# Twelve more blocks of the second product as three rounded products, and another order of the first 41 blocks' steps

## The chip, the cores and the metric

One core of a Trainium2 chip runs the whole program. The metric is the device time of one execution in microseconds (us). The kernel before takes 478.98 us, the median of three executions (477.38 to 479.07 us).

## What is computed

A gated recurrence over 768 positions for 4 batches and 8 heads of size 40 gives a matrix x of 3072 tokens by 320. A two-layer network follows: x times w_in (320 by 2048), a smooth ReLU, and the result times w_out (2048 by 320). Cut to what matters:

```python
m_new = np.maximum(f_gate[:, :, t] + m, i_gate[:, :, t])
C = f_stab * C + i_stab * np.einsum('bhd,bhe->bhde', vt, kt)
n = f_stab * n + i_stab * kt
y[:, :, t] = o * np.einsum('bhde,bhe->bhd', C, qt) / np.maximum(np.abs(nq), 1.0)
...
h = x @ w_in
g = np.where(h >= 1, h, np.where(h <= -1, 0.0, (h + 1) ** 2 / 4))
return (g @ w_out).astype(np.float32)
```

## The kernel before

**The recurrence in sequences.** The recurrence is cut into 24 sequences n (6 chunks of 128 positions times 4 batches; sequence n is chunk n // 4 of batch n % 4). For each of them TensorE multiplies queries and keys (`score_mm`, step C, tile `raw`), ScalarE makes the decays (`decay`, D, tile `Abc`), VectorE multiplies the two (`score_mul`, c), TensorE takes the product with the values (`values_mm`, U), and VectorE adds the part that comes from the state (`values_add`, u, tile `hv`), makes the normalizer (z, three small instructions), the gated result (s and y, tiles `sz` and `y`; for four sequences GpSimd does these as t and n). TensorE turns the result (T, tiles `ident,y`), ScalarE and VectorE write its high and low parts (x, and w with two instructions, tiles `xh` and `xl`). The state is kept beside it: K on TensorE (`v,vk`, or `ow` in the first chunk), k, i and a on VectorE (tile `C`, and `hv<-psa,G` for i), I on TensorE (`C,qn`), e, E, v and S on GpSimd.

**The network in blocks.** Four sequences make a group of 512 tokens, and 16 blocks of 128 hidden columns belong to each group, which makes 96 blocks x. `mm1` (step M, tile `psh`) is 8 products of 512 columns (7 where `narrow` has done one), in a rounded float32 format with a high and a low part of both sides. ScalarE and VectorE make the ReLU in three steps (R and q on ScalarE, r, which is `sharpen`, on VectorE, tile `r`). `mm2` (step N, tile `pso`) is the second product: for each of the four 128-token tiles either one plain float32 product of `rs` and `of`, or three rounded ones with `gh`, `gl` and `oh`, `ol`. `gh` is made by ScalarE (`high`, step G) and `gl` by VectorE (`low`, step g). Which of the two it is depends on whether step G has run for the block:

```python
        if x in gh:
            prod = [(gh[x], oh[:, fc, :]), (gh[x], ol[i][:, k, :]), (gl[x], oh[:, fc, :])]
        else:
            prod = [(rs[x], of[i][:, k, :])]
```

In the kernel before the first G in the order is G16, so blocks 0 to 15 (the whole first group) are plain and 80 blocks are split.

**The weights.** They arrive as 64-bit numbers in 16 pieces of two blocks each and are put into float32 by `convert`, whose steps are the digits 1 (ScalarE, tile `mg`), 2 and 5 (VectorE), 3 (GpSimd), 6 (ScalarE, the high part, `wh` or `oh`) and 7 (VectorE, the low part, `wl` or `ow`). The number behind the digit is the piece: 0, 1, 3, 5, 7, 9, 11, 13 are of w_in (tiles `win`), 2, 4, 6, 8, 10, 12, 14, 15 of w_out (tile `ow`). A split second product needs steps 6 and 7 of its w_out piece, a plain one needs steps 1 to 5 alone.

**What sets the order.** The text ORDER lists all steps by hand; every engine runs its part of them in that order (class `InOrder`), with waits only where data need them. "+n" behind a step puts n products of zeros, which compute nothing, ahead of its first TensorE instruction (`hot`). `ps_h` has two buffers, so M of a block waits for r of the block two M before it. `wk`, `mo` and `ow` are pools of buffers in SBUF; `stage` holds the pieces in work and is closed before the pool `late` opens at the first step p.

Of the kernel before, what the change touches and what calls it, by code (L numbers as in the profile page):

```python
# [42 lines left out]
15 35 B8 c4.1 P1 v5 55 R4 L6 S5 q4 r4 Q5 D5.1 N2 65 16 c4.0 75 26 L7 36 A6 D5.0 B9 q5 L8 N3 Z1 U4 u4 z4 L10 r5 t4 n4
M6 R6 C5 q6 E5 56 27 S6 17 c5.1 N4 T4 x4 66 I5 c5.0 r6 37 M7 e4 w4 57 I6 i6 A7 D6.0 Q6 e6 V7 N5 K5 R7 67 i5 28 38 S7
L9 77 D6.1 210 U5 a4 M8 E6 310 q7 18 r7 D7.0 M9 C6 Q7 u5 z5 64 k5 58 A9 L11 R8 q8 e5 c6.1 N6 L12 c6.0 110 510 t5 a5 U6
29 r8 n5 D7.1 H0 u6 T5 R9 62 19 N7 39 x5 59 69 v6 K6 z6 V8 t6 v7 q9 w5 L13 79 k6 a6 A8 N8 L14 C7 M10 211 c7.0 A10 111
r9 E7 c7.1 311 n6 511 M11 R10 Q9 V9 611 112 610 212 711 I7 T6 R11 312 i7 q10 Q8 S8 x6 N9 213 q11 113 U7 M12 M13 512
r10 w6 u7 e7 D8.1 E8 313 R12 r11 q12 L15 513 613 K7 X6 68 N10 R13 N11 k7 X4 z7 t7 I8 713 114 n7 T7 V10 q13 v8 S10 M14
R14 214 M15 314 x7 S9 r12 q14 r13 514 N12 N13 i8 614 r14 w7 I9 72 215 K8 D9.1 M16 315 115 515 N14 i9 74 M17 X5 R15 X7
76 p8 78 q15 r15 R16 a7 D8.0 612 C8 q16 k8 615 710 712 r16 N15 P2 c8.1 D10.1 M18.1 R17 c8.0 e9 O0.0 G16 O0.1 D10.0  # L50
o0.1 q17 m8 b8 o0.0 J9.18 D9.0 g16 R18 l8 r17 G17 M19 Q10 U8 N16 c9.0 c9.1 O0.2 q18 r18 R19 e8 M20.1 O0.3 m9 b9 q19
714 E9 j10.20 r19 u8 g17 G18 Z2 N17 Q12 p9 z8 l9 M21 R20 q20 c10.1 G19 v9 c10.0 A11 U9 s8 a8 v10 y8 K9 E10 M22 o0.2
r20 o0.3 V11 I10 715 R21 q21 k9 u9 r21 T8 x8 G20 z9 g18 R22 Q11 M23 A12 N18 R23 g19 p10 l10 m10 G21 i10 w8 g20 q22 q23
r22 N19 G22 b10 a9 I11 e11 S11 e10 A13 U10 g22 N20 g21 E11 s9 r23 M24 u10 D11.1 D11.0 z10 N21 G23 X8 R24 s10 y9 q24
y10 M25 r24 i11 G24 S13 g23 T9 R25 g24 N22 x9 S12 q25 w9 X9 D13.0 r25 K10 N23 k10 v11 V12 a10 G25 D12.0 g25 J11.26 N24
D12.1 c11.0 c11.1 U11 K11 u11 E12 N25 z11 V13 v12 k11 A14 s11 T10 p12 P3 M26 x10 y11 l12 D13.1 w10 X10 a11 T11 M27 x11
R26 w11 X11 q26 I12 R27 r26 I13 S14 q27 i12 M28.1 i13 G26 r27 e12 D14.0 g26 e13 j12.28 G27 M29 c12.0 Q13 R28 g27 Q14
q28 c12.1 Z3 N26 r28 m12 M30 b12 G28 N27 R29 g28 q29 K12 R30 r29 N28 v13 V14 q30 k12 G29 a12 M31 g29 r30 G30 N29 R31
g30 q31 M32 r31 G31 g31 I14 R32 M33 e14 q32 D14.1 r32 U12 G32 M34 R33 u12 E13 g32 q33 z12 N30 R34 r33 q34 s12 p13 M35
G33 r34 l13 g33 y12 N31 R35 i14 q35 r35 M36.1 O1.3 O1.2 G34 o1.3 o1.2 g34 j13.36 R36 q36 M37 c13.1 Q15 O1.1 c13.0 o1.1  # L60
O1.0 T12 R37 m13 o1.0 N32 q37 r36 b13 x12 r37 K13 G35 w12 X12 N33 V15 k13 v14 g35 U13 G37 a13 g37 K14 E14 u13 N34 k14
V16 z13 A15 v15 A16 p14 I15 G36 s13 N35 l14 g36 e15 y13 M38 a14 i15 N36 R38 q38 S15 r38 M39.1 G38 D15.1 g38 S16 j14.39
R39 M40 c14.1 Q16 q39 c14.0 D16.1 r39 T13 m14 K15 R40 M41 v16 k15 q40 b14 x13 r40 N37 R41 w13 X13 q41 D15.0 r41 U14
N38 u14 E15 G40 z14 G39 V17 D16.0 g40 J15.42 g39 M42 G41 s14 Q17 c15.1 A17 c15.0 N39 R42 g41 q42 y14 a15 U15 r42 T14
u15 E16 A18 M43 x14 z15 S17 w14 X14 s15 I16 R43 y15 P4 M44 e16 q43 i16 D17.1 r43 p16 S18 T15 M45.1 x15 R44 w15 X15 l16
q44 J16.45 R45 r44 q45 N40 c16.0 Q18 Z4 r45 c16.1 M46 m16 N41 b16 G43 G42 g43 M47 G44 g42 D18.0 g44 N42 R46 q46 U16
R47 r46 q47 N43 u16 E17 A19 D18.1 r47 z16 M48 p17 G46 s16 l17 G47 g46 D17.0 N44 g47 S19 R48 M49.1 q48 G45 r48 D19.1
g45 j17.49 M50 c17.0 Q20 R49 c17.1 q49 m17 N45 R50 q50 r49 b17 r50 K16 M51 k16 V18 v17 N46 R51 q51 r51 M52 G48 a16 g48
N47 R52 q52 M53 r52 O2.3 O2.1 o2.3 G49 o2.1 G51 g49 I17 M54.1 e17 g51 R53 i17 q53 O2.0 D19.0 J18.54 r53 o2.0 O2.2 M55
H1 o2.2 Q19 c18.0 c18.1 N48 H2 H3 H4 U17 G50 y16 H5 g50 N49 E18 u17 R55 z17 R54 A21 I18 s17 q55 N50 i18 e18 G52 y17  # L70
q54 g52 H6 T16 r54 K17 x16 H7 M56 v18 V19 k17 H8 S21 H9 w16 X16 N51 R56 H10 a17 q56 r55 K18 G54 H11 M57 G53 V20 k18
v19 g54 g53 N52 H12 R57 r56 q57 I19 G56 r57 N53 e19 g56 i19 M58 N54 M59 G55 G57 g55 g57 R58 T17 H13 N55 x17 q58 w17
X17 H14 r58 R59 K19 p18 N56 q59 m18 l18 D21.1 r59 b18 M60 G58 G59 g58 N57 R60 g59 q60 a18 D21.0 r60 U18 k19 N58 a19
E19 G60 u18 V21 g60 M61.1 A20 z18 s18 y18 j19.61 R61 q61 M62 c19.1 c19.0 r61 U19 R62 G61 S20 q62 g61 T18 A22 M63 x18
r62 E21 D20.1 w18 X18 u19 N59 p21 R63 z19 l21 q63 s19 D20.0 I21 r63 P5 N60 S22 y19 G63 i21 D22.1 g63 C20 N61 c20.1 Q22
G62 c20.0 Q23 D22.0 g62 T19 I20 x19 N62 i20 Z5 w19 X19 M64 N63 R64 q64 M65.1 O3.2 O3.1 r64 o3.1 o3.2 G64 j22.65 R65
g64 q65 M66 c22.1 Q21 r65 O3.3 O3.0 M67 R66 c22.0 o3.0 o3.3 q66 G65 r66 N64 R67 g65 q67 G66 r67 J21.68 g66 G67 N65
c21.1 c21.0 g67 M68 m21 N66 R68 b21 q68 r68 M69 G68 g68 N67 R69 q69 r69 M70 G69 g69 N68 R70 q70 r70 M71 G70 g70 N69
R71 q71 r71 U21 G71 N70 u21 E20 g71 V22 z21 M72 V23 p20 A23 s21 l20 m20 N71 R72 y21 q72 b20 r72 M73 G72 g72 U20 R73
q73 M74 u20 E22 r73 z20 S23 G73 I22 R74 p22 T21 g73 l22 M75 x21 s20 q74 w21 X21 D23.0 y20 N72 i22 R75 m22 q75 T20 N73  # L80
r74 b22 x20 r75 G74 w20 X20 G75 M76 g74 D23.1 g75 U22 R76 q76 M77.1 u22 E23 r76 z22 G76 j23.77 R77 g76 q77 s22 M78
c23.1 c23.0 r77 N74 R78 y22 q78 r78 M79 G77 g77 I23 R79 T22 i23 q79 N75 x22 r79 w22 X22 U23 G78 g78 N76 u23 z23 s23
N77 G79 y23 g79 T23 N78 x23 w23 X23 M80 N79 R80 q80 r80 M81 O4.1 O4.2 G80 o4.1 o4.2 g80 M82 R81 q81 r81 O4.3 R82 M83
# [846 lines left out]
```

## Time and profile before

| | |
|---|---|
| median of three executions | 478.98 us |
| the profiled execution | 479.52 us, of it span 477.7 us |
| TensorE (PE) busy | 468.7 us, 98% of the span |
| VectorE (DVE) busy | 322.5 us, 68% |
| ScalarE (ACT) busy | 286.5 us, 60% |
| GpSimd (POOL) busy | 154.3 us, 32% |
| granted TensorE clock | 1.0 in all 40 slices |
| DMA | 51.69 MB, mean 108 GB/s |

A row of the profile names an instruction by what it writes and reads: `gl<-r,gh` is the low part of step g, `pso<-ow,r` a plain second product (two records for each), `pso<-oh,gh`, `pso<-ow,gh` and `pso<-oh,gl` the three products of a split one. All rows have the helper's line L111, so they are told apart by tiles. A TensorE record lasts longer than the engine needs for it, since products overlap; what one costs in a stream is the distance from its start to the next one's.

### The profile page before, as it was taken

Reading aid. Unit: us, or ns where it says so; the run is one execution under the profiler, and the core shown is the slowest. Engines: PE = TensorE matmul, PEld = TensorE weight load, DVE = VectorE, ACT = ScalarE, POOL = GpSimd, SP = SyncE. Lnnn points to the kernel's source line nnn. Section 1 sums busy time; section 2 is a strip of 40 time slices with the busy share of each in tenths; the row PEclk is TensorE's granted clock in tenths of the full one; section 3 lists DMA queues with packets and bytes.
Section 4 is the critical chain, followed back from the end, with each engine's and each line's share of the span. In section 5 each row is a group of like instructions: output and inputs, shape, how many; then the busy total and the mean of one; then the engine's idle time right before and its main releaser. Section 6 shows DMA issues by size and latency. Waiting matters only on the chain.

```text
span 477.7 us, 8809 instructions
## 1 busy us (share of the span) xinstructions
PE 468.7 (98%) x3399; PEld 404.6 (85%) x3399; DVE 322.5 (68%) x582; ACT 286.5 (60%) x559; POOL 154.3 (32%) x175
## 2 busy tenths in 40 slices
...
GB/s 267 296 206 274 244 199 284 214 198 94 96 113 112 45 174 67 2 128 132 81 162 29 73 72 102 89 0 128 116 127 0 89 1 1 1 56 0 1 0 56
DMA packets 25433, 51.69 MB, mean 108 GB/s; under 512 B 8312, under 2 KB 14896, under 8 KB 25392
## 3 DMA queue, kind: packets, MB, share of 16 engines
...
## 4 chain that ended last, share of the span: by engine, by line
PE 91%; DVE 6%; DMA 1%; issue 1%; POOL 1%; ACT 0%; SPq 0%; DVEq 0%; POOLq 0%
PE pso L111 38%; PE psh L111 37%; PE psa L111 16%; DMA ident<-in_cst 1%; DVE win L111 1%; DVE C L111 1%; DVE z L111 1%; POOL fi_s L111 1%; DVE xl L111 0%; DVE y L111 0%; DVE r L111 0%; DVE xh L111 0%; DVE sz L111 0%; DVE hv L111 0%; ACT r L111 0%
## 5 line engine op out<-in xcount | busy, mean ns | idle before, releaser
L111 ACT ACTIVATE r<-psh,half 128x512 f32<-128x512 f32 x96 | 65.8, 686 | 90.4 <-PE psh L111 87.8
L111 PE MATMUL psh<-xh,wh 128*128 128x512 f32 x288 | 102.8, 411 | 1.2 <-DVE r L111 0.8
L111 PE MATMUL pso<-oh,gh 128*128 128x320 f32 x320 | 101.7, 318 | 0.0
L111 DVE SCALAR_TENSOR_TENSOR r<-psh,r 128x512 f32<-128x512 f32 x96 | 65.7, 686 | 52.3 <-ACT r L111 51.6
L111 PE MATMUL pso<-ow,gh 128*128 128x320 f32 x320 | 99.0, 309 | 0.0
L111 PE MATMUL pso<-oh,gl 128*128 128x320 f32 x320 | 98.8, 309 | 0.0
L111 PE MATMUL psh<-xh,wl 128*128 128x512 f32 (+1 forms) x274 | 94.0, 400 | 0.0
L111 DVE TENSOR_TENSOR gl<-r,gh 128x512 fp32r<-128x512 f32 x80 | 62.4, 791 | 28.0 <-ACT gh L111 27.8
L111 ACT CAST gh<-r 128x512 fp32r<-128x512 f32 x80 | 48.7, 616 | 46.2 <-DVE r L111 25.6
L111 PEld LDWEIGHTS pso<-oh,gh 128*128 128x128 f32 x320 | 60.2, 188 | 3.1 <-issue 0.5
L111 PEld LDWEIGHTS pso<-ow,gh 128*128 128x128 f32 x320 | 60.3, 188 | 2.0
L111 ACT ACTIVATE r<-r 128x512 f32<-128x512 f32 x96 | 60.5, 631 | 2.3
L111 PEld LDWEIGHTS psh<-xh,wl 128*128 128x128 f32 (+1 forms) x274 | 51.3, 188 | 12.1 <-DVE wl L111 0.2
L111 PE MATMUL psh<-xl,wh 128*128 128x512 f32 x192 | 60.6, 397 | 0.0
L111 PEld LDWEIGHTS pso<-oh,gl 128*128 128x128 f32 x320 | 60.1, 188 | 0.0
L111 PEld LDWEIGHTS psh<-xh,wh 128*128 128x128 f32 x288 | 49.2, 189 | 9.8 <-DVE r L111 2.0
L111 ACT ACTIVATE Abc<-Abc,nA 128x128 f32<-128x128 f32 x160 | 50.7, 390 | 2.5 <-POOL Abc L111 2.3
L111 POOL TENSOR_TENSOR v<-vk,G 128x328 f32<-128x328 f32 x36 | 29.6, 825 | 64.9 <-PE psa L111 45.2
L111 POOL TENSOR_TENSOR m<-m 128x1024 bf16<-128x1024 f32 x12 | 24.2, 2017 | 60.4 <-DVE m L111 50.7
L111 PEld LDWEIGHTS psh<-xl,wh 128*128 128x128 f32 x192 | 36.1, 188 | 8.9 <-DVE xl L111 0.4
L111 DVE TENSOR_TENSOR Abc<-psa,Abc 128x512 f32<-128x512 f32 x43 | 28.1, 684 | 15.6 <-PE psa L111 15.3
L111 PE MATMUL pso<-ow,r 128*128 128x320 f32 x128 | 36.9, 436 | 0.0
...
## 6 DMA issues: line engine op xcount, KB each, us to landing
...
```

The lines of the kernel that those rows point to most:

```text
L111: r = getattr(self.engine, name)(*args, **kwargs)
```

## The change

Blocks 0 to 3 stay plain; blocks 4 to 15 get steps G and g, and with them the split second product. The w_out pieces from the third on get their float32 form in one buffer of `stage` in place of one of `ow` each, since only the high and low parts are used later. To make room, the single gate chunk of later on (steps H) shares its tiles with the batch of gates before it, and `dx` shares one with `ex`. The order of the steps is another one up to `c16.0 Q18`, between M45 and M46; behind it both texts are the same. The instructions that are added are 12 `gh` casts on ScalarE and 12 `gl` subtractions on VectorE; on TensorE 48 plain products become 144 rounded ones, and 32 products of zeros become 26. No conversion, transfer or step of the recurrence is added or left out.

```diff
@@
-SPLIT_FROM = 8
+PLAIN = 2
@@ def gate_sums(c):
-        new = lambda name, p, n=L: pool.tile([p, n], F32, name=name if c else name + "0", bufs=1)
+        def new(name, p, n=L):
+            if c and name != "ex":
+                shared = pool.tile([P, NB * L + 1 if name == "m" else L], F32, name={"m": "m_s"}.get(name, name + "_u"), bufs=1)
+                return shared[:p, :n]
+            return pool.tile([p, n], F32, name=name if c else name + "0", bufs=1)
+
@@ def batch_exps():
-        batch["dx"] = later.tile([P, D], F32, name="dx", bufs=1)
+        batch["dx"] = later.tile([P, L], F32, name="ex", bufs=1)[:, :D]
@@ def convert(k, nw):
             if k == 2:
-                w["out"] = of[i] = ow.tile([P, 656], F32, name="ow")[:, :2 * DM].rearrange("p (k e) -> p k e", k=2)
+                if i < PLAIN:
+                    of[i] = ow.tile([P, 656], F32, name="ow")[:, :2 * DM]
+                else:
+                    of[i] = stage.tile([P, 2 * DM], F32, name="wout", bufs=1)
+                w["out"] = of[i] = of[i].rearrange("p (k e) -> p k e", k=2)
@@ ORDER
...
-v2 w3 11 Lc K1 M0 V4 21 F R0 31 k0 B4 V3 B5 K2 k1 51 q0 M1 k2 61 v3 I4 L2 R1 r0 q1 71 22 32 r1 B6 A4 B7 i4 M2 12 52 M3
-K3 R2 L3 23 v4 k3 A5 R3 33 13 53 K4 q2 N0 L4 E4 63 q3 N1 r2 S4 D4.0 73 M4 D4.1 k4 r3 24 V5 M5 L5 14 C4 34 54 25 R5 V6
...
+K2 s3 y3 B4 B5 w2 T3 w0 x3 L2 w3 V3 12 61 V4 w1 F A4 M0 R0 k0 B6 q0 B7 L3 v3 k1 22 M1 k2 P1 32 v4 R1 q1 r0 I4 Z1 71 52
+23 A5 K3 r1 L4 M3 k3 S4 N0 13 M2 i4 33 53 24 Q4 R3 q3 r3 N1 L5 63 K4 L6 R2 q2 14 34 E4 S5 73 54 A6 D4.1 k4 Q5 25 L7 r2
...
```

**First place: VectorE ahead of the first block.** The rows show VectorE's queue at the end of the front, where the low parts of the first four turned results (`xl`, `xh`) are made, which the first M needs. Before:

```order
L111 TENSOR_TENSOR y<-pso,sz 128x320
L111 TENSOR_TENSOR xl<-psa,xh 128x2x128
...
L111 TENSOR_TENSOR xl<-pso,xh 128x2x128
L111 TENSOR_TENSOR xh<-pso,xh 64x128
L111 TENSOR_SCALAR win<-wraw 128x768
L111 TENSOR_TENSOR C<-psh,cs 120x369
L111 SCALAR_TENSOR_TENSOR fi_s<-fi_s,ah_u 128x128
L111 SCALAR_TENSOR_TENSOR ah_u<-rst,fi_s 128x128
L111 TENSOR_TENSOR C<-pso,cs 120x369
L111 SCALAR_TENSOR_TENSOR win<-mg,win 128x768
```

In the change:

```order
L112 TENSOR_SCALAR win<-wraw 128x768
L112 TENSOR_TENSOR A_295<-pso,A_295 128x512
...
L112 TENSOR_TENSOR y<-pso,sz 128x320
L112 SCALAR_TENSOR_TENSOR win<-mg,win 128x768
...
L112 TENSOR_TENSOR y<-psa,sz 128x320
L112 SCALAR_TENSOR_TENSOR fi_s<-fi_s,ah_u 128x128
L112 SCALAR_TENSOR_TENSOR ah_u<-rst,fi_s 128x128
L112 TENSOR_TENSOR xl<-psh,xh 128x2x128
L112 TENSOR_TENSOR xh<-psh,xh 64x128
```

The two VectorE steps of weight piece 1 (21 and 51, tile `win`) and the gate sums of step B4 (`fi_s`, `ah_u`) stand ahead of the low parts now; they stood behind them.

**Second place: TensorE around blocks 4 and 5.** The rows show second products among first products, values and turns. Before:

```order
L111 MATMUL psa<-raw 128x128 x8
L111 MATMUL pso<-ow,r 128x320 x4
L111 MATMUL psa<-v_925,Abc 128x41 x8
L111 MATMUL psa<-ident,y 128x128 x3
L111 MATMUL pso<-ow,r 128x320 x4
```

In the change:

```order
L112 MATMUL psa<-raw 128x128 x8
L112 MATMUL pso<-oh,gh 128x320
L112 MATMUL pso<-ow,gh 128x320
L112 MATMUL pso<-oh,gl 128x320
...
L112 MATMUL psa<-v_980,Abc 128x41 x8
L112 MATMUL psa<-ident,y 128x128 x3
```

Where four plain products stood for a block, twelve rounded ones stand (three for each of the four token tiles).

**Third place: VectorE behind the values of sequence 5.** The rows begin with step u5 (`hv<-psa,hv`) in both. Before:

```order
L111 TENSOR_TENSOR hv<-psa,hv 128x328
L111 SCALAR_TENSOR_TENSOR z<-hv,G 128x8
L111 TENSOR_TENSOR z<-z,hv 128x8
L111 RECIPROCAL z<-z 128x8
L111 TENSOR_TENSOR C<-psa,cs 120x369
L111 SCALAR_TENSOR_TENSOR ow<-mg,ow 128x640
L111 TENSOR_TENSOR Abc<-psa,Abc 128x512 x2
L111 SCALAR_TENSOR_TENSOR ow<-mg,ow 128x640
L111 TENSOR_TENSOR C<-C 120x369
L111 TENSOR_SCALAR win<-wraw 128x768
```

In the change:

```order
L112 TENSOR_TENSOR hv<-psa,hv 128x328
L112 TENSOR_SCALAR wout<-wraw 128x640
L112 TENSOR_TENSOR C<-psa,cs 120x369
...
L112 TENSOR_TENSOR gl<-r,gh 128x512
L112 TENSOR_TENSOR Abc<-psa,Abc 128x512
...
L112 SCALAR_TENSOR_TENSOR wout<-mg,wout 128x640
...
L112 TENSOR_TENSOR ow<-wout,oh 128x640
L112 TENSOR_TENSOR gl<-r,gh 128x512
```

The subtractions `gl` and the low parts of w_out (`ow<-wout,oh`) stand among the same work of the recurrence, where before only steps 2 and 5 of w_out stood; before, the steps 7 of w_out came some ten blocks later.

## Rows read from the trace of the kernel before

**Rows 1.** The page: busy time by engine, and the chain that ended last.

```profile
PE 468.7 (98%) x3399; PEld 404.6 (85%) x3399; DVE 322.5 (68%) x582; ACT 286.5 (60%) x559; POOL 154.3 (32%) x175
...
PE 91%; DVE 6%; DMA 1%; issue 1%; POOL 1%; ACT 0%; SPq 0%; DVEq 0%; POOLq 0%
```

**Rows 2.** Stretches: length, busy us (x instructions) of PE, PEld, DVE, ACT, POOL, clock, DMA.

```profile
66.30:91.50 25.20, 25.07 (x155) 19.92 (x154) 22.12 (x36) 16.20 (x34) 16.24 (x17) 1.00 0.80 262
...
130.00:157.90 27.90, 27.90 (x258) 25.14 (x257) 26.45 (x44) 16.62 (x29) 16.79 (x15) 1.00 0.34 100
42.00:130.00 88.00, 87.87 (x534) 68.86 (x533) 66.89 (x110) 62.60 (x128) 49.76 (x49) 1.00 0.65 204
```

**Rows 3.** Timeline (start us, us), two plain second products, then I, K and a first product.

```profile
108.88 4.47 PE L111 MATMUL pso<-ow,r 128*128 128x320 f32 x16
113.19 0.79 PE L111 MATMUL psa<-C,qn 120*128 120x123 f32 x6
113.82 0.83 PE L111 MATMUL psa<-v,vk 128*120 128x123 f32 x6
114.41 0.48 PE L111 MATMUL psh<-xh,wh 128*128 128x512 f32 x1
```

**Rows 4.** Timeline: a split second product, a first product, the next split one.

```profile
441.44 0.31 PE L111 MATMUL pso<-oh,gh 128*128 128x320 f32 x1
...
443.19 0.63 PE L111 MATMUL psh<-xh,wh 128*128 128x512 f32 x2
...
445.06 0.31 PE L111 MATMUL pso<-oh,gh 128*128 128x320 f32 x1
```

**Rows 5.** Timeline of VectorE and TensorE where the first blocks begin.

```profile
31.73 0.29 DVE L111 TENSOR_TENSOR xh<-pso,xh 64x128 fp32r<-64x128 f32 x1
32.05 0.62 DVE L111 TENSOR_SCALAR win<-wraw 128x768 uint16<-128x768 uint16 x1
...
32.79 0.79 PE L111 MATMUL psa<-ow 128*120 128x123 f32 x6
33.16 0.28 DVE L111 SCALAR_TENSOR_TENSOR fi_s<-fi_s,ah_u 128x128 f32<-128x128 f32 x1
33.39 0.70 PE L111 MATMUL psh<-xh,wh 128*128 128x512 f32 x2
33.48 0.42 DVE L111 TENSOR_TENSOR_SCAN ah_u<-rst,fi_s 128x128 f32<-128x128 f32 x1
...
34.25 1.07 DVE L111 SCALAR_TENSOR_TENSOR win<-mg,win 128x768 int32<-128x768 int32 x1
...
36.64 0.33 PE L111 MATMUL psa<-ident,fi_s 128*128 128x128 f32 x1 [0.40 <-POOL fi_s L111]
```

**Rows 6.** Timeline: VectorE idle in the front.

```profile
27.14 0.17 DVE L111 SCALAR_TENSOR_TENSOR z<-pso,G 128x8 f32<-128x8 f32 x1 [1.08 <-PE pso L111]
```

**Rows 7.** Timeline: score products (C), values (U), a turn (T) and what follows it.

```profile
10.80 1.16 PE L111 MATMUL psa<-raw 40*128 40x128 f32 x16
...
15.96 1.98 PE L111 MATMUL psa<-ow,Abc 128*128 128x41 f32 x16
...
104.81 0.49 PE L111 MATMUL psa<-ident,y 128*128 128x128 f32 x3
105.05 0.71 PE L111 MATMUL psh<-xh,wh 128*128 128x512 f32 x2
```

**Rows 8.** Step g on VectorE: min/median/max ns from 260 us; busy, mean from 122 to 160.

```profile
L111 DVE TENSOR_TENSOR gl<-r,gh x51: 677/692/2276, 265.1 to 469.9; 128x512 fp32r<-128x512 f32 x51
...
L111 DVE TENSOR_TENSOR gl<-r,gh 128x512 fp32r<-128x512 f32 x9 | 9.1, 1033 | 0.3 <-ACT gh L111 0.3
```

**Rows 9.** Step 2 of w_in on VectorE: its mean from 42 to 122 us, and two single ones.

```profile
L111 DVE TENSOR_SCALAR win<-wraw 128x768 uint16<-128x768 uint16 x5 | 4.9, 990 | 0.0
...
85.91 1.47 DVE L111 TENSOR_SCALAR win<-wraw 128x768 uint16<-128x768 uint16 x1
...
92.19 0.60 DVE L111 TENSOR_SCALAR win<-wraw 128x768 uint16<-128x768 uint16 x1
```

More of the change, by code (lines that the diff above doesn't have):

```diff
@@ L43 @@
[L43 to L82, printed above, removed]
@@ L83 @@
[L83 to L87 removed]
+Lg fg1 Eb0 fg2 fg3 P0 Z0 Li fs+6 L0 Q0 Ab0 D0.0 Lv0 Eb2+3 fg4+3 Lf C0+3 Ab2 Q1 E0 20 30 Eb1+1 c0.0 D0.1 Ab1 c0.1 B0
@@ new lines @@
+G5 D5.1 66 n4 M7 27 17 R6 g4 g5 76 N4 A7 q6 18 T4 E5 37 L10 R7 c5.1 N5 c5.0 x4 57 67 r6 28 38 Q6 58 w4 77 68 D6.1 v5
+I5 i5 I6 M8 K5 e4 L9 U5 Q7 L11 i6 S7 a4 G6 q7 r7 78 V7 g6 D6.0 u5 e6 Q8 D7.0 M9 210 e5 E6 G7 k5 C6 310 R8 z5 g7 N6
+c6.0 q8 t5 a5 c6.1 U6 110 510 r8 n5 T5 N7 29 L12 610 u6 z6 19 39 710 R9 V8 L13 L14 G8 g8 v6 V9 x5 v7 K6 N8 59 69 w5 C7
+k6 79 211 q9 r9 t6 c7.0 111 A9 D7.1 311 511 M10 c7.1 212 R10 n6 q10 M11 r10 I7 611 L15 i7 112 64 E7 U7 G10 G9 711 312
+T6 R11 q11 g10 M12 213 u7 g9 K7 x6 z7 512 R12 r11 N9 a6 t7 w6 612 113 k7 712 q12 G11 313 M13 R13 214 314 513 g11 613
@@ new lines @@
+x8 G21 u9 m10 M23 p10 z9 r22 G20 w8 l10 b10 s9 X8 S11 R23 q23 Q12 k9 U10 D11.1 v10 y9 M24 r23 V11 G23 g20 N20 I11 e9
+u10 g21 E11 R24 q24 G22 i11 A12 z10 g22 s10 g23 T9 N21 r24 M25 a9 N22 D11.0 x9 S12 e10 y10 D12.0 w9 K10 Q11 R25 q25
+N23 G24 S13 k10 g24 o0.2 r25 G25 J11.26 a10 c11.0 o0.3 c11.1 N24 v11 K11 k11 U11 u11 g25 D13.0 T10 x10 D13.1 V12 D12.1
+z11 s11 y11 M26 R26 N25 w10 q26 T11 x11 V13 v12 M27 R27 q27 I12 A14 w11 I13 H0 e12 r26 M28.1 i12 e11 r27 G26 X9 g26
+j12.28 R28 q28 P3 i13 a11 r28 G28 g28 M29 c12.0 E12 Q13 c12.1 M30 G27 g27 R29 N26 K12 k12 R30 a12 N27 N28 q29 r29 q30
```

45 lines of the change are left out of this document (38 added, 7 removed).

## The prediction

> **What bounds the kernel now.** I read the page first, then busy time by stretches, then single steps in order of time. The page says TensorE: it is busy for 468.7 of 477.7 us and makes up 91% of the chain that ended last [rows 1]. A busy TensorE need not be an engine at its pace, so the stretch in which the change works has to be seen by itself. From 42 to 130 us, which runs from the second product of block 0 to that of block 16, TensorE is busy for 87.87 of 88.00 us, while VectorE works for 66.89 us, 76% [rows 2]. The products also stand at their own distances there: two plain second products start at 108.88 and the next step at 113.19 [rows 3]. So nothing waits, and every us that TensorE is spared in this stretch could shorten the whole. The reader should keep the two other numbers of that row in mind: VectorE has 21 us of idle time in 88, and GpSimd works for 49.76 us, 57%, which is far more than its 32% of the whole span [rows 1, 2].
>
> **Term a, the second products of blocks 4 to 15.** A plain one takes (113.19 - 108.88) / 2 = 2.155 us [rows 3]. A split one starts at 441.44 and the next step at 443.19, 1.75 us, with twelve weight loads that hide behind the products [rows 4]. The difference is 0.405 us, twelve times of it 4.9 us. Both kinds stand on the critical engine, so all of it would show: **-4.9 us**, with 4.3 us as the low end if the split ones, among other small products, lose 0.05 us each.
>
> **Term b, the front.** The order before block 0 is another. Many steps swap places and cost the same; what counts is what stands ahead of the low parts of the first x, since the first M needs them. The last low part ends at 32.02 [rows 5]. Three pieces of VectorE work stood behind it and stand ahead of it now: the two steps of weight piece 1 (0.62 and 1.07 us) and the gate sums (0.28 and 0.42 us), 2.4 us in all [rows 5]. Given back later: the state product at 32.79, which takes 0.60 us to the next step, is done earlier by the change, and the turn of the gates, for which TensorE idles 0.40 us at 36.64, has its input sooner [rows 5]. That leaves 1.4 us. Part of the moved work falls into a wait: VectorE idles 1.08 us for the values of sequence 3 before 27.14 [rows 6], and in the change piece 1 stands right there. If all of that wait is filled, 0.3 us remain; I take the middle, **+0.8 us**, with 0.3 and 2.4 as ends. I leave out a gain, since the first decays still wait for the same gate inputs and scans. The identity matrix is loaded ahead of the first weight piece now, but I count nothing for it: in the new order the gate tail stands ahead of the first use of the turned gates on VectorE. The 6 products of zeros that go lie in waits of the front and are counted as nothing; if the waits behind them shrink, that is in the ends.
>
> **Term c, VectorE between blocks 5 and 11.** The change adds 12 steps g, and it moves the low parts of six w_out pieces ten blocks forward, into the stretch where the weights are still put into float32. From the moment at which the values of sequence 5 are there (VectorE cannot run ahead of them) to the end of g of block 11, VectorE's queue holds 50 instructions: 5 g, 4 r, 4 c, 15 of weights, 22 of the recurrence. In the densest stretch of before, 130.00 to 157.90, with GpSimd as busy as here, 44 instructions take 26.45 us, 0.601 each [rows 2]. The 50 then take 30.1 us. TensorE has in the same stretch, up to the second product of block 11, five M of 1.87 us [rows 4], five N of 1.75, two score products of 1.16, two values products of 1.98, two turns of 0.24 [rows 7], two I of 0.63 and two K of 0.59 [rows 3]: 9.35 + 8.75 + 2.3 + 4.0 + 0.5 + 1.3 + 1.2 = 27.4 us. With 0.2 us at each end for the handover (an estimate, half of the 0.40 us idle of [rows 5]) VectorE is 30.1 + 0.4 - 27.4 = **3.1 us** too long, and N of block 11 waits so much longer. What queues behind: r of the next block stands after g, and M of the block after next waits for r, so nothing of TensorE can slip past. ScalarE's 12 added casts I count at nothing: it works 62.60 of 88 us [rows 2] and its queue has no such pile. The transfers that move with their steps (weight pieces, keys and queries, the gates of steps H on SP's queue) count as nothing as well: the DMA engines are busy for 0.65 of the stretch from 42 to 130 us, 0.80 at its fullest part [rows 2], and no load is added; what one late piece would cost is in the ends of c.
>
> The ends of c: nothing, if VectorE's queue is no longer than TensorE's; that needs 0.54 us for each instruction, and single ones do get so short (step 2 of w_in at 92.19 takes 0.60 us where the mean is 0.99 [rows 9]). Above, the five g take 1.033 us as from 122 to 160 us and not the 0.692 of later [rows 8], +1.7 us, and the three steps 2 of w_in take 1.47 us [rows 9], +1.4 us: 6.2 us. I take 3.1, because the dense stretch is nearest in its mix. After block 11 the queue relaxes, since fewer pieces are left, and the time lost is not won back: TensorE has no waits to shrink.
>
> One thing of rows 8 deserves a second look. The same subtraction takes 0.677 to 2.276 us. In the Trainium skill, "SBUF — State Buffer", section "SBUF: two separate sides", it is said that VectorE and GpSimd share a pair of ports, held for a whole instruction by whoever starts first, also against a VectorE instruction with two SBUF inputs. Step g has two such inputs, and the trace agrees in so far as g is long where GpSimd is busy (1.033 us in the mean where GpSimd works 60%, against a median of 0.692 later). By that rule each added g could be held up and the sum would go to the second rival's end; by the means of the dense stretch it stays at 3.1 us, and I follow those.
>
> **The sum.** -4.9 + 0.8 + 3.1 = -1.0 us, made against the profiled execution of 479.52 us (span 477.7 us), which lies 0.5 us above the median. From the median of 478.98 us this gives **478.0 us**. Everything from block 42 on is the same in both and is carried along. A measurement of this kernel can tell about 0.5% from no change, 2.4 us; the forecast lies within that.
>
> **The rivals.**
>
> *VectorE keeps up.* The order was laid out so that every g stands well ahead of its N; if pieces overlap better than in the dense stretch, c is nothing and b 0.6 us. For it: VectorE idles 24% from 42 to 130 us, and in the dense stretch it is 95% busy without TensorE waiting [rows 2]. Against it: the 50 instructions need more than the time there is. Result: -4.9 + 0.6 = -4.3, **474.7 us**. Chance 0.31.
>
> *VectorE is held up by GpSimd.* The place is the stretch of blocks 5 to 11, where GpSimd's selects, conversions and scalings run beside g and the weights' steps; the mechanism is that these take as long as their long rows and not as their mean. For it: GpSimd at 57 to 64% of the stretches [rows 2], the 1.033 and 1.47 us rows [rows 8, 9]. Against it: in 66.30 to 91.50, where both are busy, VectorE still gets 36 instructions done in 22.12 us, 0.614 each, hardly more than elsewhere [rows 2]. It decides once b and c together exceed 4.9 us, and counts as slower by over 0.5% once they exceed 7.3 us. At c = 6.2 and b = 2.0 the sum is +3.3, **482.3 us**. Chance 0.15. The Trainium skill's section on the two sides of SBUF, named above, is the rule that would bring this about; it changes nothing in the number.
>
> *The forecast.* Term c between 0.7 and 5.5 us with term b as above, -3.4 to +1.4 us. Chance 0.54, of which 0.02 lie below the bound of 0.5% and 0.01 above it in single measurements.
>
> That the change does not do what it says I leave out: the order of TensorE's instructions shows 16 plain second products where there were 64, the other 48 as three rounded ones each.
>
> **How the numbers follow.** Faster by over 0.5% is the first rival and 0.02 of the forecast, 0.33; slower by over 0.5% is the second rival and 0.01 of the forecast, 0.16; within 0.5% is the rest, 0.51. The range takes in the first rival's time and most of its bound (-4.9 + 0.3 = -4.6, 474.4 us) and stops short of the second's at 481.8 us. The forecast's own range alone runs from 475.6 to 480.4 us.
>
> **What would show it.** In the profile of the change: second products of blocks 4 to 15 at 1.75 us each; the step behind the first M some 2 us later than its 32.79 us [rows 5], with about half of that caught up by the second product of block 0; idle TensorE, or late starts after `gl` and `r`, of some 3 us in blocks 8 to 11 (about 80 to 105 us); VectorE at over 90% from 65 to 105 us. The forecast is wrong if g of those blocks lies ready before its N (first rival), if g there takes over 1.1 us in the mean or TensorE waits over 6 us (second rival), or if TensorE waits at a place that I have not named, such as behind ScalarE's casts.

## The result, and the profile after

| | before | change |
|---|---|---|
| median | 479.02 us (4 executions) | 473.75 us (472.67 to 487.48, 4 executions) |
| ratio | | 0.9888, 95% interval 0.985 to 0.9925 |
| profiled execution | 479.52 us, span 477.7 us | 472.67 us, span 470.9 us |

The change is 5.3 us faster, 0.65 us below the low end of the forecast's range. The 487.48 us are an execution with a mean granted clock of 0.967, which the ratio leaves out.

The page of the change, with the row of busy times that answers to [rows 1]:

```profile
PE 463.4 (98%) x3441; PEld 408.0 (87%) x3441; DVE 328.8 (70%) x594; ACT 293.3 (62%) x571; POOL 156.2 (33%) x175
```

TensorE is busy for 5.3 us less with 42 records more, VectorE for 6.3 us more. The two stretches that answer to [rows 2]: from the second product of block 0 to that of block 16, and from step u5 to the end of g of block 11, which is the stretch of term c:

```profile
38.58:123.51 84.93, 84.84 (x546) 73.30 (x544) 79.58 (x126) 67.04 (x131) 51.33 (x46) 1.00 0.63 197
71.28:99.10 27.82, 27.82 (x196) 25.28 (x195) 27.24 (x51) 18.54 (x32) 18.38 (x17) 1.00 0.66 214
```

VectorE went from 76% to 94% between blocks 0 and 16 and has 0.6 us left in 27.8 in the second stretch. TensorE shows no wait there; what VectorE's added work costs it all the same is measured below, against the run without g. Now single steps of the change: a split second product (block 9, 92.77 to 94.61), the front, and the step at which both orders have done the same work (M0 to M3, N0, N1, K0 to K4, I4):

```profile
26.26 0.95 DVE L112 SCALAR_TENSOR_TENSOR win<-mg,win 128x768 int32<-128x768 int32 x1
27.13 0.16 DVE L112 SCALAR_TENSOR_TENSOR z<-psa,G 128x8 f32<-128x8 f32 x1
...
29.01 0.42 DVE L112 TENSOR_TENSOR_SCAN ah_u<-rst,fi_s 128x128 f32<-128x128 f32 x1
...
32.04 0.29 DVE L112 TENSOR_TENSOR xh<-psa,xh 64x128 fp32r<-64x128 f32 x1
...
33.10 0.38 PE L112 MATMUL psa<-ident,fi_s 128*128 128x128 f32 x2
...
45.30 0.71 PE L112 MATMUL psh<-xh,wh 128*128 128x512 f32 x2
...
92.77 0.39 PE L112 MATMUL pso<-oh,gh 128*128 128x320 f32 x1
...
94.61 0.39 PE L112 MATMUL psh<-xh,wh 128*128 128x512 f32 x1
```

The last low part (32.04) ends 0.3 us later than in [rows 5], although 2.4 us of VectorE work moved ahead of it; the turn of the gates at 33.10 follows its predecessor without a wait. Before, the state of 45.30 is reached 0.87 us later. This is one pair of traces: four runs below that keep the change's front come to the second product of block 0 at 38.44 to 39.02 us where the change has 38.58, so up to 0.4 us of it can be chance. A wait that the prediction did not name lies at the turn of sequence 15, inside the reordered part. Timeline of the kernel before:

```profile
46.17 0.86 PE L111 MATMUL psh<-xh,wh 128*128 128x512 f32 x2
...
245.34 1.11 DVE L111 TENSOR_TENSOR sz<-sig,z 128x320 f32<-128x320 f32 x1
246.48 1.31 DVE L111 TENSOR_TENSOR y<-hv,sz 128x320 f32<-128x320 f32 x1
...
243.46 1.01 DVE L111 TENSOR_TENSOR z<-z,hv 128x8 f32<-128x8 f32 x1
...
243.36 1.09 POOL L111 TENSOR_SCALAR_AFFINE_SELECT Abc<-Abc 128x1024 f32<-128x1024 f32 x1
...
245.30 0.80 POOL L111 TENSOR_TENSOR C<-C,dec 120x369 f32<-120x369 f32 x1 [0.49 <-PE psa L111]
246.36 1.09 POOL L111 TENSOR_SCALAR_AFFINE_SELECT Abc<-Abc 128x1024 f32<-128x1024 f32 x1 [0.25 <-DMA Abc<-a_d]
...
247.94 0.52 PE L111 MATMUL psa<-ident,y 128*128 128x128 f32 x3 [0.88 <-DVE y L111]
248.97 0.73 PE L111 MATMUL psh<-xh,wh 128*128 128x512 f32 x2 [0.52 <-DVE r L111]
```

The same turn in the change:

```profile
238.23 0.49 DVE L112 TENSOR_TENSOR sz<-sig,z 128x320 f32<-128x320 f32 x1
238.75 1.06 DVE L112 TENSOR_TENSOR y<-hv,sz 128x320 f32<-128x320 f32 x1
...
238.67 0.80 POOL L112 TENSOR_TENSOR C<-C,dec 120x369 f32<-120x369 f32 x1 [7.56 <-PE psa L112]
...
240.61 0.52 PE L112 MATMUL psa<-ident,y 128*128 128x128 f32 x3
240.88 0.40 PE L112 MATMUL pso<-oh,gh 128*128 128x320 f32 x1
```

Before, a select of GpSimd (243.36, step S17) stands beside one of the normalizer's three instructions, `z` at 243.46 (1.01 us); `sz` (1.11 us) begins late by it and falls beside the state decay (245.30, step e16), and `y` (1.31 us) beside the next select (246.36). TensorE waits 0.88 and 0.52 us. In the change `z` takes 0.17 us (at 236.75) and `sz` 0.49 us with no GpSimd instruction beside them, while `y` stands beside the decay (238.67) and takes 1.06 us. TensorE shows no wait, and a second product stands behind the turn, so the wait for r is gone too.

**Where the 6.8 us between the two spans lie**, by the starts of the same steps: -0.87 us up to the state of 45.30; -5.11 us at the second product of block 24 (158.45 against 163.56), so 4.24 us lie between; -6.36 us at that of block 42 (252.92 against 259.28), the turn of sequence 15 in between; -6.8 us at the end. What of the 4.24 us is the split and what VectorE costs can't be read from this pair, since the order differs too; two of the experiments part them. The profiled execution of the change is the lowest of its four and that of before 0.5 us above its median, hence 6.8 in the spans and 5.3 in the medians.

### The profile page after: what moved, and what is told of

It is laid out like the page before. It is cut to its first block, busy times and chain, and to the rows that moved or that the text cites. A ratio compares the mean times of both kernels' runs of the same rounds, so it can differ in the third digit from the quotient of the medians.

```text
span 470.9 us, 8937 instructions
## 1 busy us (share of the span) xinstructions
PE 463.4 (98%) x3441; PEld 408.0 (87%) x3441; DVE 328.8 (70%) x594; ACT 293.3 (62%) x571; POOL 156.2 (33%) x175
## 4 chain that ended last, share of the span: by engine, by line
PE 90%; DVE 7%; ACT 1%; issue 1%; POOL 0%; POOLq 0%; DVEq 0%
PE psh L112 37%; PE pso L112 37%; PE psa L112 16%; DVE win L112 1%; DVE r L112 1%; DVE wout L112 1%; ACT r L112 1%; DVE gl L112 1%; DVE C L112 1%; DVE Abc L112 1%; DVE ow L112 0%; DVE z L112 0%; DVE wl L112 0%; DVE xl L112 0%; DVE sz L112 0%
## 5 line engine op out<-in xcount | busy, mean ns | idle before, releaser
L112 PE MATMUL pso<-oh,gh 128*128 128x320 f32 x368 | 116.5, 317 | 0.0
L112 PE MATMUL pso<-oh,gl 128*128 128x320 f32 x368 | 113.8, 309 | 0.0
L112 PE MATMUL pso<-ow,gh 128*128 128x320 f32 x368 | 113.5, 309 | 0.0
L112 DVE TENSOR_TENSOR gl<-r,gh 128x512 fp32r<-128x512 f32 x92 | 71.3, 784 | 28.3 <-ACT gh L112 27.7
L112 ACT CAST gh<-r 128x512 fp32r<-128x512 f32 x92 | 55.7, 616 | 41.9 <-DVE r L112 24.0
L112 PEld LDWEIGHTS pso<-oh,gh 128*128 128x128 f32 x368 | 69.1, 188 | 3.5 <-ACT gh L112 0.5
L112 PEld LDWEIGHTS pso<-ow,gh 128*128 128x128 f32 x368 | 69.2, 188 | 2.2
L112 PEld LDWEIGHTS pso<-oh,gl 128*128 128x128 f32 x368 | 69.1, 188 | 0.4 <-DVE gl L112 0.3
L112 POOL TENSOR_SCALAR_AFFINE_SELECT Abc<-Abc 128x1024 f32<-128x1024 f32 x20 | 25.9, 1294 | 15.4 <-DMA Abc<-a_d 11.8
```

Source lines behind the costliest of these rows:

```text
L112: r = getattr(self.engine, name)(*args, **kwargs)
```

## The experiments

Each is compared with the kernel before on the same chip (medians 479.1 to 479.4 us). The first theory was: the split pays as priced, and the change's order lets VectorE keep up. The rivals: the order pays by itself, or VectorE had room all along. Lines of the order are shown cut at both ends.

**Plain products in blocks 4 to 15, steps G and g kept.**

```diff
-        if x in gh:
+        if 4 <= x < 16:
+            prod = [(rs[x], ol[i][:, k, :].bitcast(F32))]
+        elif x in gh:
```

(The plain products take the low part of w_out as their right side, so this kernel computes those blocks with other weights, at the cost of a plain one.)

> The change, but blocks 4 to 15 take one plain product per token tile again (of the kept tile ow, so the output is not the reference's), while steps G and g of these blocks still run and nobody reads them. Theory 1 (the split itself pays, 0.405 us a block): 12 x 0.405 = 4.9 us slower than the change, 478.6 us. Rival (the new order pays, and the split is paid for by VectorE): within 1 us of the change, 473 to 475 us.

476.6 us, ratio 0.9954 (0.9935 to 0.9972). Between the two: the split, net of what VectorE costs it, is worth 2.9 us of the 5.3 in the medians and 4.0 in the spans (474.9 against 470.9 us); 2.5 us (2.8 in the spans) come from the order, with G and g in it.

**No g.**

```diff
+        if 4 <= x < 16:
+            gl[x] = gh[x]
+            return
         gl[x] = mo.tile([P, TT], F32R, name="gl", bufs=3)
```

The low parts of blocks 4 to 15 are left out, `gh` stands in for them.

> The change without the 12 added subtractions of step g on VectorE (the third product of blocks 4 to 15 reads gh in place of gl, so the output is not the reference's; TensorE's work is the same). Theory 1 (VectorE just keeps pace between blocks 5 and 11): 0 to 0.7 us faster than the change, 473.0 to 473.7. Rival (VectorE is the bound there, as the prediction had it, and the gain comes from elsewhere): 2 to 4 us faster, 470 to 472.

472.15 us, ratio 0.9863 (0.9841 to 0.9884). The twelve g cost 1.6 us in the medians, 0.7 us in the spans (470.2 against 470.9). Between the two expectations; VectorE has no room to give away, but it is not 3 us too long either.

The change, the plain products and the run without g have the same order of TensorE's steps, so their traces can be compared stretch by stretch. Here they are in this order, from the second product of block 4 to that of block 16, which holds all twelve blocks (columns as in [rows 2]):

```profile
61.68:123.51 61.83, 61.74 (x420) 55.57 (x418) 57.37 (x96) 46.67 (x93) 37.05 (x34) 1.00 0.59 192
62.00:127.68 65.68, 65.68 (x372) 52.00 (x370) 58.01 (x96) 46.55 (x93) 36.56 (x34) 1.00 0.59 180
61.81:122.73 60.92, 60.92 (x419) 55.02 (x418) 49.99 (x86) 46.24 (x93) 35.57 (x34) 1.00 0.61 194
```

Without g the split saves 65.68 - 60.92 = 4.76 us, which is term a by itself (with plain products TensorE is busy throughout, so g costs nothing there). The twelve g cost 61.83 - 60.92 = 0.91 us, which is term c by itself. Together 3.85 us are left.

**Five g more**, each of blocks 6 to 10 made twice.

```diff
-g6
+g6 g6
...
-g10
+g10 g10
```

> The change with step g of blocks 6 to 10 done twice (and G with no second time): 5 more subtractions of some 0.69 us on VectorE, 3.5 us. If VectorE is at its edge between blocks 5 and 11: 2.5 to 3.5 us slower than the change, 476.3 to 477.3. If it has slack there: within 0.7 us of it.

477.59 us, ratio 0.9962 (0.9942 to 0.9982): 3.8 us more, about what five g of 0.69 us take (3.5 us). The timeline shows where TensorE stops, in the middle of the second product of block 8:

```profile
82.62 0.41 PE L112 MATMUL pso<-oh,gl 128*128 128x320 f32 x1 [1.33 <-DVE gl L112]
```

VectorE has no idle time from 69.53 to 82.49 us there, so it is the length of its queue that ends late, and not a buffer of `gl` that is missing. The change stands at VectorE's edge, and 0.9 us beyond it: all that is added shows, and little is won by taking work away. This is the point where the forecast's term c begins.

**S17 behind e16 in the kernel before**, as the change has it.

```diff
-z15 S17 w14 X14 s15 I16 R43 y15 P4 M44 e16 q43
+z15 w14 X14 s15 I16 R43 y15 P4 M44 e16 S17 q43
```

> The kernel before with one step moved: GpSimd's selection of sequence 17 (S17) behind the state decay e16, so that it no longer runs beside the normalizer and the gated result of sequence 15 on VectorE. Theory (the 1.7 us that TensorE waits at 246.66 to 248.97 come from VectorE being slow beside GpSimd): that wait falls below 0.5 us, and the time is 1.2 to 1.7 us below before, 477.3 to 477.8. Rival (the turn of sequence 15 is late for another reason): no change in that wait, 479.0.

478.62 us, ratio 0.9988 (0.9978 to 0.9998), span 476.8 against 477.7 us. The profile shows the turn without a wait:

```profile
243.31 0.17 DVE L111 TENSOR_TENSOR z<-z,hv 128x8 f32<-128x8 f32 x1
...
244.35 0.49 DVE L111 TENSOR_TENSOR sz<-sig,z 128x320 f32<-128x320 f32 x1
244.87 0.49 DVE L111 TENSOR_TENSOR y<-hv,sz 128x320 f32<-128x320 f32 x1
...
246.74 0.49 PE L111 MATMUL psa<-ident,y 128*128 128x128 f32 x3
246.99 0.71 PE L111 MATMUL psh<-xh,wh 128*128 128x512 f32 x2
```

With the select gone from beside it, `z` takes 0.17 instead of 1.01 us. `sz` begins 1.0 us sooner, and `sz` and `y` (0.49 us each) begin before the decay (245.14) and end before the selects start (245.98). 0.6 us in the medians and 0.9 in the spans come out of it, less than the 1.2 to 1.7 us expected: a new wait of TensorE of 0.32 us for r stands at 249.61. A part of what the order pays is shown here.

**The old front with the change's rest**, and **the new front with the rest of before.**

```diff
-Lg fg1 Eb0 fg2 fg3 P0 Z0 Li fs+6 L0 Q0 Ab0 D0.0 Lv0 Eb2+3
...
-w2 T3 w0 x3 L2 w3 V3 12 61 V4 w1 F A4 M0 R0 k0 B6 q0
+Lg fg1 fg2 P0 Z0 ht+7 L0 20 30 Li Eb0+7 fs Ab0 Eb1+3 D0.1
...
+w3 11 Lc K1 M0 21 31 51 K2 B4 B5 L2 V3 12 61 V4 F A4 R0 k0 B6 q0
```

> The change with the order of before up to the first M; the 13 steps that the change has done by then (two steps of weight piece 1, the gate sums and others) follow right behind it. If the new front is what made the state behind the second product of block 1 come 0.9 us sooner: 0.5 to 1.5 us slower than the change. If the prediction's term b were right (the old front has the first blocks sooner): 0.5 to 1 us faster than the change.

> The kernel before with the change's order up to the first M, and the rest of before behind it. If the new front is worth something by itself: 0.5 to 1.5 us below before, 477.5 to 478.5. If the prediction's term b is right: 0.3 to 1.4 us above before.

Old front: 477.28 us, ratio 0.9962 (0.9944 to 0.9979), 3.5 us more than the change, far more than expected. New front: 478.59 us, ratio 0.9983 (0.9962 to 1.0004), 0.5 us less than before, 1.0 us in the span; the interval does not exclude that it gains nothing. The old front loses at the turn of the gates, which the change's rest puts right behind the first M. Timeline of the old front, then busy time by stretches (columns as in [rows 2], the clock behind the five engines):

```profile
35.11 0.33 PE L112 MATMUL psa<-ident,fi_s 128*128 128x128 f32 x1 [1.50 <-POOL fi_s L112]
36.72 0.33 PE L112 MATMUL psa<-ident,fi_s 128*128 128x128 f32 x1 [1.28 <-POOL fi_s L112]
...
34.03 0.43 DVE L112 TENSOR_TENSOR_SCAN ah_u<-rst,fi_s 128x128 f32<-128x128 f32 x1
```

```profile
32.00:36.00 4.00, 1.94 (x11) 1.38 (x10) 3.77 (x9) 2.14 (x4) 1.32 (x3) 1.00 0.49 172
36.00:40.00 4.00, 3.28 (x13) 2.72 (x14) 2.93 (x5) 1.56 (x6) 3.76 (x6) 0.76 0.78 320
40.00:44.00 4.00, 4.00 (x22) 3.56 (x22) 2.65 (x4) 3.94 (x5) 3.84 (x4) 0.82 0.54 166
```

The gate sums end at 34.46 instead of 29.43 us, GpSimd turns them into `fi_s` only then, TensorE idles for half of 32 to 36 us, and behind that the granted clock falls to its lower level for a part of 36 to 44 us. Three of the ten executions kept a clock of 1.000 there (475.48 to 476.25 us), the seven with 0.992 to 0.996 took 477.17 to 479.21 us.

**The pieces behind the low parts in the change** (21, 31, 51, B4, B5, 12, 61).

```diff
-y1 70 21 31 c3.0 V0
+y1 70 c3.0 V0
...
-y3 B4 B5 w2 T3 w0 x3 L2 w3 V3 12 61 V4 w1 F A4 M0
+y3 w2 T3 w0 x3 L2 w3 V3 V4 w1 21 31 51 B4 B5 12 61 F A4 M0
```

> The change with the two steps of weight piece 1 and the gate sums on VectorE (and what hangs on them on ScalarE and GpSimd) behind the low parts of the first x, as they stood before. The prediction's reasoning (2.4 us of VectorE's work ahead of the first M delay it): the step behind the first M starts 1.5 to 2.4 us sooner than at 33.10 us, and the time is 0 to 1.5 us below the change, 472.3 to 473.7. Rival (these steps filled idle VectorE): the step behind the first M at 33.10 within 0.5 us, and the time the same or up to 1 us above, since the gates' turn waits.

478.43 us, ratio 0.9991 (0.9971 to 1.001): 4.7 us more than the change. The profiled execution took 492.19 us, so its trace names the place and not the size. The waits of TensorE from 28 to 60 us:

```profile
PE psa L112 <- POOL fi_s L112: 3.4, 2, 2.1
```

It is the place at which the old front waits, and the other executions have a mean clock of 0.993 to 0.996, as the old front's have. The pieces are not a burden that the change bears, its rest needs them early. Both expectations missed this.

**The split put into the order of before**, G and g some twelve steps ahead of each N, the w_out pieces' steps 6 and 7 right behind step 5.

```diff
+G4 g4 M6 R6 C5 q6 E5 56 66 76 27 S6
...
+L9 77 D6.1 U5 a4 M8 E6 q7 18 r7 D7.0 M9 C6 Q7 u5 z5 64 G6 g6
```

> The split of blocks 4 to 15 with the order of before: G and g of these blocks are put in some 12 steps ahead of their second product, and the high and low parts of the six w_out pieces right behind step 5 of each; all else as before. If the split alone brings its 4.9 us whatever the order: 474.1 us. If a new order is needed to pay for it (VectorE and ScalarE queues late for N): 476 to 481 us, with TensorE waiting for gh or gl between blocks 4 and 16.

500.88 us, ratio 1.0461 (1.0436 to 1.0486). The longest of TensorE's waits from 45 to 135 us, and one stretch of them:

```profile
PE psh L112 <- DVE r L112: 6.7, 3, 3.3
```

```profile
124.00:130.00 6.00, 3.01 (x9) 2.13 (x8) 2.72 (x4) 2.85 (x6) 1.82 (x2) 0.78 0.14 56
```

The queues stall each other: first products wait for r, which stands behind other work. A part of the 21.8 us is the clock's, which was granted at 0.78 in the stretch shown. The 4.9 us of term a are not to be had in the order of before with the steps merely put in; other ways to put them in were not tried.

**The change's opening alone in the kernel before, up to the first values product.**

```diff
-Lg fg1 fg2 P0 Z0 ht+7 L0 20 30 Li Eb0+7 fs Ab0 Eb1+3 D0.1 D0.0 10 Ab1 Q0
...
+Lg fg1 Eb0 fg2 fg3 P0 Z0 Li fs+6 L0 Q0 Ab0 D0.0 Lv0 Eb2+3 fg4+3 Lf C0+3 Ab2 Q1 E0 20 30 Eb1+1 c0.0 D0.1 Ab1 c0.1 B0 U0+1
...
```

> The kernel before, with the change's opening alone: the steps up to the first values product U0 stand in the change's order (gate tail and gate exponentials ahead of the second half of the first decays, the first step of weight piece 0 behind them), everything behind in the order of before. Theory (the front of the change gains at its opening and gives a part back with the pieces ahead of the low parts): in the change's trace the first score multiplication starts at 11.24 us instead of 13.57 us, 2.3 us sooner, and no VectorE work is put in front of the low parts here, so the first M starts 1.0 to 2.3 us sooner than its 30.62 us and the time is 476.8 to 478.1 us against 479.1 us. Rival (the first x waits for something behind the opening, such as the loads or the gate maxima): less than 0.4 us, 478.7 to 479.2 us.

490.18 us, ratio 1.0241 (1.0228 to 1.0254): the cut brought a wait of its own and says nothing about the opening. It shows what a wait of this length costs, in all five executions (mean clock 0.978 to 0.982):

```profile
22.49 3.61 PE L111 MATMUL psh<-ow,Abc 128*128 128x41 f32 x16 [3.72 <-DVE Abc L111]
```

```profile
20.00:24.00 4.00, 1.51 (x8) 1.54 (x8) 2.34 (x5) 0.00 (x0) 1.66 (x3) 0.50 0.91 332
...
36.00:40.00 4.00, 4.00 (x19) 3.46 (x19) 2.31 (x8) 0.74 (x2) 0.00 (x0) 0.50 0.00 0
```

**The pieces alone in the kernel before**, which is term b by itself.

```diff
-c3.0 U3+3 y1 T0 z2 s2 z3 L1 T1+2 B3 y2 T2 v0 s3 y3 x0 x2 w0
+L1 c3.1 11 U2+1 V2 c3.0 U3+3 y1 T0 21 31 z2 s2 z3 T1+2 B3 y2 T2 v0 51 s3 y3 B4 B5 x0 x2 w0
```

> The kernel before, with the other half of the change's front alone: the two VectorE steps of weight piece 1 and the gate sums stand ahead of the low parts of the first x (steps L1, 11, 21, 31, 51, B4 and B5 moved), the opening stays. This is term b of the prediction by itself. As predicted: +0.8 us (0.3 to 2.4), 479.4 to 481.5 us against 479.1 us, with the last low part at 32.3 to 34.4 us instead of 32.02 us. Rival (these steps fall into waits of VectorE in the front, and the turn of the gates and the weights come sooner): no loss, 478.0 to 479.1 us.

480.18 us, ratio 1.002 (1.001 to 1.0031): 0.9 us more, where the prediction said 0.8. The number agrees, but the trace has a loss in it that the prediction did not mean:

```profile
26.44 0.62 DVE L111 TENSOR_SCALAR win<-wraw 128x768 uint16<-128x768 uint16 x1 [2.26 <-DMA wraw<-in_w_in]
...
34.31 0.29 DVE L111 TENSOR_TENSOR xh<-pso,xh 64x128 fp32r<-64x128 f32 x1
```

The last low part ends at 34.60 us, against 32.02 us before [rows 5], and the first M starts at 33.20 instead of 30.62 us; 1.7 us of that are won back later. VectorE idles 2.26 us for the load of weight piece 1, which this order issues at 15.61 us; the change issues it at 12.22 us, and there the same step runs at 23.07 us without a wait. So the 0.9 us are the price of the pieces and of a late load together, and no run parts the two.

**g of blocks 6, 8 and 10 on GpSimd.**

```diff
-        nc.vector.tensor_tensor(out=gl[x], in0=rs[x], in1=gh[x].bitcast(F32), op=ALU.subtract)
+        eng = nc.gpsimd if x in (6, 8, 10) else nc.vector
+        eng.tensor_tensor(out=gl[x], in0=rs[x], in1=gh[x].bitcast(F32), op=ALU.subtract)
```

> The change, with the low parts gl of blocks 6, 8 and 10 made on GpSimd instead of VectorE (the same subtraction). VectorE is at its edge between blocks 5 and 11: without any of the twelve g the time was 1.6 us shorter, with five more it was 3.8 us longer. Theory (only VectorE's length counts): three steps of 0.69 us less, and the time falls by 0.3 to 1.0 us, to 472.7 to 473.5 us. Rival (GpSimd is as near its edge, by its queue or because the two hold each other up): its selects, conversions and scalings come some 1.2 us later for each, and the time rises to 474.5 to 477 us.

> The change itself once more, so that it stands beside the three others on the same chip: 473.3 to 474.3 us, 5 to 6 us below the kernel before.

The change again: 473.96 us, ratio 0.9882 (0.9867 to 0.9896). With three g on GpSimd: 475.88 us, ratio 0.9942 (0.9921 to 0.9963), 1.9 us more. GpSimd needs 1.55 us for one in the mean, and TensorE waits for what stands behind it there, the scaled values of a sequence:

```profile
82.24 0.90 PE L112 MATMUL psa<-v,vk 128*120 128x123 f32 x6 [2.44 <-POOL v L112]
...
79.31 1.47 POOL L112 TENSOR_TENSOR gl<-r,gh 128x512 fp32r<-128x512 f32 x1 [1.83 <-ACT gh L112]
```

**The whole new front without the pieces, in the kernel before**, the complement of the pieces alone.

```diff
-v0 K0 Lc x2 v2 51 z3 K1 K2 s3 y3 B4 B5 w2 T3 w0 x3 L2 w3 V3 12 61 V4 w1 F A4 M0
+v0 K0 Lc x2 v2 z3 K1 s3 y3 w2 T3 w0 x3 w3 w1 M0 V4 21 F R0 31 k0 B4 V3 B5 K2 k1 51
```

(The removed line is the change's, the added one this kernel's.)

> The kernel before with the change's whole front up to the first M, but without the steps that the change draws ahead of the low parts (21, 31, 51, B4, B5 and what hangs on them stay behind the first M as before). Together with the run in which only those were drawn forward, which took 0.9 us more than before, it makes up the change's front, which with the rest of before took 0.5 us less. Theory (the front's gain lies in its opening, the part that the prediction left out, and the pieces take their 0.9 us from it): 1.2 to 2.2 us less than before, 477.0 to 478.0 us, the first M 1.3 to 2.5 us sooner than its 30.62 us. Rival (the gain comes from the pieces and the opening being moved together, since the earlier opening leaves waits in which the pieces fit): no gain from the opening alone, 478.7 to 479.5 us.

479.04 us, ratio 1.0006 (0.9993 to 1.0019): no gain, the rival holds.

```profile
29.91 0.73 PE L111 MATMUL psh<-xh,wh 128*128 128x512 f32 x2 [0.57 <-ACT xh L111]
...
36.20 0.33 PE L111 MATMUL psa<-ident,fi_s 128*128 128x128 f32 x1 [0.41 <-POOL fi_s L111]
...
27.02 0.17 DVE L111 SCALAR_TENSOR_TENSOR z<-psa,G 128x8 f32<-128x8 f32 x1 [0.93 <-PE psa L111]
```

The first M starts 0.7 us sooner than before, but the turn of the gates waits as in [rows 5] and VectorE idles 0.93 us for the values of sequence 3 as in [rows 6]. In the change's own rows above, the second step of piece 1 (26.26) fills that idle time. In these runs neither half of the front pays alone: the pieces +0.9 us (with the late load in it), the rest nothing. Both together show -0.5 us with the rest of before, not clear of noise, and 3.5 us with the change's rest, much of which the old front loses at the turn of the gates.

**One of the pieces later in the change** (51 behind the low parts, 61 behind R0).

```diff
-x2 v2 51 z3 K1 K2 s3 y3 B4 B5 w2 T3 w0 x3 L2 w3 V3 12 61 V4 w1 F A4 M0 R0
+x2 v2 z3 K1 K2 s3 y3 B4 B5 w2 T3 w0 x3 L2 w3 V3 12 V4 w1 51 F A4 M0 R0 61
```

> The change with one VectorE step less ahead of the first M: the second step of weight piece 1 (51, 0.95 us) stands behind the low parts, its high part (61) behind the first ReLU step; the gate sums stay ahead. In the change's trace the first M waits 0.57 us for the high part and 0.64 us for a low part of x. Theory: the low parts end 0.9 us sooner, both waits shrink, and since VectorE has no idle time to speak of from there to block 11 the step only changes place: 0 to 0.8 us less than the change, 473.0 to 473.9 us. Rival (the third block's weights, whose low part ends just as its products begin, come late): 0.5 to 1.5 us more, 474.3 to 475.3 us.

475.98 us, ratio 0.9933 (0.9913 to 0.9953): 2.0 us more than the change's 473.96. The step that was free in a wait of VectorE stands in the way behind it. The trace also holds a wait for a load, which comes ahead of the moved step and which neither expectation named:

```profile
10.99 0.48 PE L112 MATMUL pso<-raw 40*128 40x128 f32 x2 [0.88 <-DMA raw<-in_qk]
...
28.48 0.17 DVE L112 SCALAR_TENSOR_TENSOR z<-psa,G 128x8 f32<-128x8 f32 x1 [0.78 <-PE psa L112]
...
33.71 1.63 DVE L112 SCALAR_TENSOR_TENSOR win<-mg,win 128x768 int32<-128x768 int32 x1
...
36.07 0.70 PE L112 MATMUL psh<-xh,wh 128*128 128x512 f32 x2 [1.02 <-DVE C L112]
```

The first M starts at 31.59 us here, at 30.22 us in the change, so some 1.4 of the 3.1 us between the spans (474.0 against 470.9) lie ahead of the moved step and are not its doing; the rest lies behind the first M.

No run that computes the whole beats the change.

## Why the prediction was wrong

**Term a held.** It said 1.75 us for a split product and -4.9 us for twelve. Block 10 takes 1.76 us (96.47 to 98.23) and block 9, behind another kind of product, 1.84 us. By the plain products and the run without g the twelve are worth 4.76 us.

**Term c failed first: +3.1 us was said, +0.9 us is what the twelve g cost** (61.83 against 60.92 us, with and without them; 0.7 us by the whole spans, 1.6 by the medians). The failed step is the price "0.601 each" from the dense stretch "because [it] is nearest in its mix". It is not. VectorE's groups from 130 to 157.9 us in the kernel before:

```profile
L111 DVE TENSOR_TENSOR gl<-r,gh 128x512 fp32r<-128x512 f32 x6 | 7.1, 1211 | 0.3 <-ACT gh L111 0.3
...
L111 DVE TENSOR_TENSOR m<-Abc 128x1024 f32<-128x1024 f32 x2 | 2.4, 1222 | 0.7 <-PE psa L111 0.7
```

and from 71.2 to 99.1 us in the change:

```profile
L112 DVE TENSOR_TENSOR gl<-r,gh 128x512 fp32r<-128x512 f32 x5 | 3.5, 693 | 0.1
```

Six long g and two m made the dense stretch slow; in the change's stretch g takes 693 ns and there is no m, and the 50 instructions took 27.8 us, 0.556 each, beside TensorE's 27.7 us (27.4 was said). The prediction had both numbers for g, 0.692 and 1.033, and the 0.54 us at which c vanishes, and still took the mean of a stretch. Five g at 0.69 instead of 1.21 us alone are 2.6 us. With 27.8 and 27.7 us in place of 30.1 and 27.4 the prediction's own sum gives 0.5 us. Of the 0.9 us, 0.3 lie in this stretch, at the score product at 82.38, which takes 1.44 us where it takes 1.16 us without g; the other 0.6 lie behind it, at the score product at 109.97 (1.56 against 1.16 us) and just ahead of that.

**Term b had the wrong sign: +0.8 us was said, -0.87 us is in the trace, of which up to 0.4 us can be chance.** Its price agrees with the pieces alone in number only (+0.9 us, with the late load in it). The step that failed is "I leave out a gain": with the new opening the pieces fall into VectorE's wait and the turn of the gates finds its input. The prediction priced the pieces alone and left the new opening beside them at nothing; that the front costs 0.8 us is out, that it gains the whole 0.87 us is not shown.

**"TensorE has no waits to shrink" was wrong.** It was argued from 42 to 130 us, but the order changes up to block 41. The two waits at the turn of sequence 15 stood in the trace of before, 0.88 and 0.52 us; the change shows neither as a wait, and moving one GpSimd step alone brings 0.6 to 0.9 us. "Everything from block 42 on is the same" held to 0.4 us: -6.36 us there, -6.8 us at the end.

**The rival "VectorE keeps up"** comes nearest, with the mechanism for c right in the main (0.9 us where it has nothing) and 474.7 us against 473.75. That its time lies so near is partly luck: it has the front at +0.6 us, and about 2.5 us come from the order, which no rival names. The second rival did not occur: g took 693 ns in the change's stretch. Three g on GpSimd are no case of it, since there GpSimd's own queue made TensorE wait.

In one sum, in the spans: -0.87 (the front) - 4.76 (the split) + 0.91 (VectorE) - 0.39 (the order from block 0 to block 24, a remainder that no run parts) - 1.25 (blocks 24 to 42, with the turn of sequence 15) - 0.44 (behind) = -6.8 us.
